# Moving V inside one core: a queue change, a transpose on TensorE, and a new placement of steps in a fused window-attention and MLP kernel

## The chip, the cores and the metric

The kernel runs on one core of a Trainium2 chip. The metric is the device time of one execution in microseconds (us); lower is better. Three executions of the kernel before took 382.96, 375.05 and 378.85 us, median 378.85 us. The profile shown below is of a separate, profiled execution with a span of 377.6 us.

## The reference

Eight batches of attention (8 heads, 576 positions, head dimension 64) in which each position sees itself and the 63 positions before it; the result goes through two matrix products with `h - tanh(h)` between them.

```python
scores = scale * np.matmul(q, k.transpose(0, 1, 3, 2))
mask = (rel >= 0) & (rel < window)            # rel = i - j, window = 64
scores = np.where(mask, scores, -1000000000.0)
attn = softmax(scores)                        # written out in the original
x = np.matmul(attn, v).transpose(0, 2, 1, 3).reshape(B * S, H * D)   # 4608 x 512
h = x @ w_in                                  # 512 x 2048
g = h - np.tanh(h)
out = (g @ w_out).astype(np.float32)          # 2048 x 512
```

Inputs and output are float32; the kernel works in bf16 with float32 accumulation.

## The kernel before

The 4608 tokens are cut into nine chunks of 512. For each chunk c there are 16 "h" operations (`hp_mm`: four 128x512 matmuls into one PSUM bank, then a tanh on ScalarE, then a subtraction on VectorE) and 16 "y" operations (`yp_mm`: four matmuls of the second product; after each fourth one the result is stored). They are laid out by number in a table of **steps**; everything of the attention is hung into these steps by hand with `at(step, function, arguments)`. Each engine executes its own instructions in exactly the order in which the loop emits them.

```python
OPS = {}
for m in range(M):                                   # M = 16
    OPS[2 * m] = "h", 0, m
    OPS[32 + m] = "y", 0, m
    OPS[48 + m] = "h", 1, m
    OPS[66 + 2 * m if m < 15 else 95] = "h", 2, m
    OPS[63 + 2 * m if m > 1 else 64 + m] = "y", 1, m
    for c in range(3, NC):
        OPS[32 * c + 2 * m] = "h", c, m
        OPS[32 * c + 2 * m + 1] = "y", c - 1, m
# ... (cut)
for h in range(32 * NC + 32):
    op = OPS.get(h)
    # ... (cut: emit the matmuls of op, then:)
    for fn, args in items.pop(h, []):
        fn(*args)
    if op and op[0] == "h":
        g_sub(*op[1:])
```

A batch b (counted from 0, so the third to sixth batches are b = 2 to 5) has four pairs of heads; pair g = 4 b + pr. The parts for one pair are: load q, k and v from HBM (GpSimd's queue, which also converts to bf16), `cast` (a re-ordering copy), `tr` (TensorE transposes of q or k, six of 96x96, then copied out of PSUM by ScalarE and VectorE), `scores` or `hidden_scores` (with the exponential on ScalarE), masking, `pv` or `tile_pv` (the product with V), the normalisation into `xs`, and last the transpose of `xs` into `xT`, which the first product reads.

V needs two copies of each key block: the product for a window of 64 queries reads 128 keys, 64 old and 64 new, over 128 partitions. V is loaded to `vall`, copied to `vb` (`cast_v`), and then moved between partitions by DMA into `vw`, of which there are two, used by even and odd batches:

```python
def windows_v(b, j, eng):                 # both halves: 128 rows of 1040 bytes
    if j == 0:
        keys_v(b, 0, eng)
    else:
        eng.dma_start(out=vw[b % 2][:, j]..., in_=vb[8 * j - 8:8 * j + 8]...)

def keys_v(b, j, eng=nc.sync):            # the new half alone: 64 rows
    eng.dma_start(out=vw[b % 2][64:128, j]..., in_=vb[8 * j:8 * j + 8]...)

def shift_v(b, j0, j1, eng=nc.sync):      # the old half is the new half of the block before
    lo, hi = vw[b % 2][0:64, j0 + 1:j1 + 1], vw[b % 2][64:128, j0:j1]
    if eng is nc.vector:
        eng.tensor_copy(lo, hi)
    # ... (cut)
```

`xs` becomes `xT` in one of two ways:

```python
def x_tr(b, half, w0, w1, bank, eng=nc.vector):   # TensorE transposes, copied out by eng
    tp = ps[:, bank, :]...
    for w in range(w0, w1):
        nc.tensor.transpose(tp[:, w - w0, :], xs[b % 2][:, w, 2 * half:2 * half + 2, :]..., ident)
    # ... (cut: move(eng, chunk_tile(c)..., tp...), one copy for each chunk touched)

def x_dma(b):                                     # DMA transposes on SyncE's queue
    # ... (cut: one DMA for each chunk touched, transpose=True)
```

SyncE's queue carries the stores of the result, the moves of V from batch 2 on and the DMA transposes. GpSimd's queue carries the loads, most `cast`s and `cast_v` from batch 3 on. To hold loads back, GpSimd copies one element of `gT` (`pace(step)`), which waits for the subtraction of the last h operation before that step; everything later on GpSimd waits behind it.

The placement of batch 2 and of later batches before the change:

```python
at(47, cast_pair, 8, V)
at(48, cast_pair, 9, G)
at(49, lambda: [cast_v(2, pr, V) for pr in range(NP)])
at(50, lambda: [windows_v(2, j, Y) for j in range(NJ)])        # Y: SyncE's queue
# ... (cut)
for i, (g, p) in enumerate(((8, 58), (9, 59), (10, 61), (11, 63))):
    at(48 + 3 * i, tr, g, "q", 3, A, V)
    at(49 + 3 * i, tr, g, "k", 3, A)
    for j in range(3):
        at(50 + 3 * i + j, hidden_scores, g, j, 4 + (3 * i + j) % 2)
    at(p, tile_pv, g, (6, 7))
# ... (cut)
LOADS = {4: (63, 64, 72), 5: (96, 99, 102), 6: (124, 128, 114)}   # k, q, v
for g in range(3 * NP, B * NP):
    b, pr = divmod(g, NP)
    a = 8 * g - 52
    s = 32 * b - 4
    cv, ky = s - 72 + 5 * pr, s - 54
    if b == 3:
        a = (62, 67, 72, 76)[pr]
        cv, ky = 63 + pr, 67
    elif b == 4:
        a = (80, 87, 95, 102)[pr]
        cv, ky = 77 + 3 * pr, 88
    elif b == 5:
        cv, ky = 107 + 2 * pr, 114
    # ... (cut)
    at(cv, cast_v, b, pr)
    # ... (cut: casts before a, tr at a and a + 2, scores at a + 5, 7, 9, masking at a + 11)
    for i in range(3):
        at(a + 13 + i, pv, g, i)
    at(a + 15, norm, g)
    if pr == NP - 1:
        at(a + 16, x_dma, b)
    for j in range(NJ):
        if pr == 0:
            at(ky + j // 2, windows_v, b, j, Y)
```

Of the kernel before, what the change touches and what calls it, by code (L numbers as in the profile page):

```python
# [15 lines left out]
def kernel(  # L16
# [11 lines left out]
    NP = H // 2  # L28
    NJ = S // 64
# [26 lines left out]
    ps = psum.tile([128, 8, 512], F32, name="ps")  # L56
# [329 lines left out]

    def hp_mm(c, ms, split):

        outs = [ps[:, m % 3 if c < 2 else m % 2, :] for m in ms]
        for kis in ((0, 2), (1, 3)) if split else ((0, 1, 2, 3),):  # L390
            for m, hp in zip(ms, outs):
                for ki in kis:
                    nc.tensor.matmul(hp, w_in_tile(ki, m),  # L393
                                     chunk_tile(c)[:, :, ki % 2, 64 * (ki // 2):64 * (ki // 2) + 64],
                                     start=(ki == 0), stop=(ki == 3))
        for m, hp in zip(ms, outs):
            th = sm_pool.tile([128, TOK], F32, tag="th", name="th")
            nc.scalar.activation(th, hp, ACT.Tanh)  # L398
            HID[c, m] = hp, th
# [27 lines left out]
    for m in range(M):  # L427
        OPS[2 * m] = "h", 0, m
        OPS[32 + m] = "y", 0, m
        OPS[48 + m] = "h", 1, m  # L430
        OPS[66 + 2 * m if m < 15 else 95] = "h", 2, m
        OPS[63 + 2 * m if m > 1 else 64 + m] = "y", 1, m
        for c in range(3, NC):
            OPS[32 * c + 2 * m] = "h", c, m
            OPS[32 * c + 2 * m + 1] = "y", c - 1, m
        OPS[32 * NC + 2 * m + 1] = "y", NC - 1, m
# [3 lines left out]
    def at(h, fn, *args):  # L440
        items.setdefault(h, []).append((fn, args))
# [84 lines left out]
    at(34, more_constants)  # L526
    at(35, lambda: [keys_v(1, j, (G, Y)[j % 2]) for j in range(NJ)])
    at(35, load, 7, "q", G)
    for g in 8, 9, 10, 11:
        at(35, load, g, "k", G)  # L530
        at(35, load, g, "q", G)
        if g == 8:
            at(35, load_v_all, 2)
    at(36, cast_pair, 4, V)
    at(37, tr_rows, 4, "k", 3, V)
    at(38, tr_rows, 4, "q", 0, A)
# [36 lines left out]
        nc.scalar.activation(PT[g % NPT][:, 3 * grp:3 * grp + 3, :], sp, ACT.Exp, scale=scale)  # L573

    at(47, cast_pair, 8, V)
    at(48, cast_pair, 9, G)
    at(49, lambda: [cast_v(2, pr, V) for pr in range(NP)])
    at(50, lambda: [windows_v(2, j, Y) for j in range(NJ)])
    at(50, cast_pair, 10, G)
    at(52, cast_pair, 11, G)  # L580
    at(52, load_all, 3, "k")
    at(52, load_all, 3, "q")
    at(53, load_v_all, 3)
    for i, (g, p) in enumerate(((8, 58), (9, 59), (10, 61), (11, 63))):
        at(48 + 3 * i, tr, g, "q", 3, A, V)
        at(49 + 3 * i, tr, g, "k", 3, A)
        for j in range(3):
            at(50 + 3 * i + j, hidden_scores, g, j, 4 + (3 * i + j) % 2)
        at(p, tile_pv, g, (6, 7))
    at(62, x_tr, 2, 0, 0, 4, 4, V)  # L590
    at(62, x_tr, 2, 0, 4, 9, 5, A)
    at(65, x_tr, 2, 1, 0, 4, 3, V)
    at(65, x_tr, 2, 1, 4, 9, 4, A)
    for i in range(2):
        at(140 + 4 * i, more_zeros, i)

# [2 lines left out]
        last = ((b + 1) * NJ - 1)  # L599
        nc.gpsimd.tensor_copy(tick, chunk_tile(last // WPC)[0:1, last % WPC, 0, 0:1])  # L600

    LOADS = {4: (63, 64, 72), 5: (96, 99, 102), 6: (124, 128, 114)}
    for g in range(3 * NP, B * NP):
        b, pr = divmod(g, NP)
        a = 8 * g - 52
        s = 32 * b - 4
        cv, ky = s - 72 + 5 * pr, s - 54
        if b == 3:
            a = (62, 67, 72, 76)[pr]
            cv, ky = 63 + pr, 67  # L610
        elif b == 4:
            a = (80, 87, 95, 102)[pr]
            cv, ky = 77 + 3 * pr, 88
        elif b == 5:
            cv, ky = 107 + 2 * pr, 114
        elif b == 6:
            cv = 120 + 4 * pr
        at(cv, cast_v, b, pr)
        if b < 7:
            at(a - {3: 4, 5: 4}.get(b, 7), cast, g, "q")  # L620
            at(a, tr, g, "q", 3, A, V)
        else:
            at(a - 14, cast_q, g)
            at(a - 12, bounce, g, "q")
            at(a - 6, tr_dma, g, "q")
        if b < 7:
            at(a - {3: 3, 5: 6}.get(b, 5), cast, g, "k")
            at(a + 2, tr, g, "k", 3, A)
        else:
            at(a - 13, cast, g, "k")  # L630
            at(a - 11, bounce, g, "k")
            at(a - 5, tr_dma, g, "k")
        for i in range(3):
            at(a + 5 + 2 * i, scores, g, i, 4)
        at(a + 11, masking, g)
        for i in range(3):
            at(a + 13 + i, pv, g, i)
        at(a + 15, norm, g)
        if pr == NP - 1:
            at(a + 16, x_dma, b)  # L640
        for j in range(NJ):
            if pr == 0:
                at(ky + j // 2, windows_v, b, j, Y)
        if pr == 0:
            hk, hq, hv = LOADS.get(b, (s - 72, s - 68, s - 78))
            if b == 3:
                continue
            for h, f in (hv, (load_v_all, b)), (hq, (load_all, b, "q")), (hk, (load_all, b, "k")):
                at(h, pace, h)
                if b == 5:  # L650
                    at(h, behind_x, 3)
                at(h, *f)
# [50 lines left out]
```

The softmax here doesn't subtract the row's maximum and nothing guards it: scores larger than these inputs give would overflow.

## Time and profile before

| what | value |
|---|---|
| device time, median of three | 378.85 us |
| span of the profiled execution | 377.6 us |
| TensorE (PE) busy | 330.6 us, 88% |
| VectorE (DVE), ScalarE (ACT), GpSimd (POOL) busy | 199.5, 183.9, 103.5 us |
| mean TensorE clock granted in the span | 0.964 |
| PE busy from 65 to 103 us (38 us) | 29.60 us |
| PE busy from 103 to 157 us (54 us) | 41.28 us |
| PE busy from 157 to 199 us (42 us) | 34.76 us |
| PE busy from 199 to 282 us (83 us) | 79.34 us |

The three stretches up to 199 us are where batches 2 to 5 pass through the attention. The profile names an instruction by engine, line of the kernel and tiles: `PE L322` is the product with V of batches 0 to 2 (`tile_pv`), `PE L346` that of later batches (`pv`), `L393` is the first product, `L417` the second, `L267` the transposes of q and k, `vw<-vb` the moves of V. An arrow such as `<-DMA vw<-vb` behind an instruction says what ended the idle time before it. The clock is a share of full speed; at 0.5 every matmul takes twice as long.

The steps can be found in the timeline by counting the groups of four matmuls of L393 and L417: step 48 begins at 65.35 us, step 64 at 102.41, step 73 at 113.48, step 79 at 127.10, step 96 at 157.12, step 121 at 186.15.

### The profile page before, as it was taken

What the parts mean: (1) busy time and instruction counts of PE and PEld (TensorE: products, weight loads), DVE (VectorE), ACT (ScalarE), POOL (GpSimd) and SP (SyncE); (2) the same over time, 40 slices, a digit from 0 to 9 for tenths busy, and PEclk for the clock granted to TensorE, in tenths of its full rate; (3) what the DMA queues carried; (4) which work ended last, traced back from release to release, by engine and by line L of the source; (5) the groups of instructions that cost most, each with busy time, mean ns of one, the idle gap of its engine ahead of it and who ended that gap; (6) DMA issues with size and microseconds to landing.
All of it is one profiled execution on the core that took longest, in us unless ns stands there. A gap on an engine that the chain in (4) does not pass through costs nothing.

```text
span 377.6 us, 6190 instructions
## 1 busy us (share of the span) xinstructions
PE 330.6 (88%) x2402; PEld 178.9 (47%) x2402; DVE 199.5 (53%) x330; ACT 183.9 (49%) x332; POOL 103.5 (27%) x153
## 2 busy tenths in 40 slices
PE   7879896796896878699849999999699999999996
PEld 3645444353453444355425555555345544444442
DVE  4557658653634358466605677666466534343400
ACT  3546264582564355366515666665355344444321
POOL 8811373402173800053507435351000000000000
PEclk9999999897999699899988999999999999999999
DMA  9999999193098107595496869768971401001012
GB/s 163 168 204 211 176 192 173 16 224 70 2 170 158 36 5 131 105 150 96 70 201 96 159 109 157 143 105 156 200 190 57 91 29 58 28 28 57 28 56 85
DMA packets 54654, 42.98 MB, mean 114 GB/s; under 512 B 23232, under 2 KB 48320, under 8 KB 54624
## 3 DMA queue, kind: packets, MB, share of 16 engines
q0 software_dynamic: 20816, 18.73, 32.6%
q1 hardware_dynamic: 33456, 23.42, 27.2%
q10 hardware_dynamic: 352, 0.43, 0.5%
q8 instruction: 19, 0.31, 0.3%
q14 instruction: 11, 0.09, 0.1%
HBM read 36.70 MB, written 11.21 MB: 127 GB/s over the span
## 4 chain that ended last, share of the span: by engine, by line
PE 61%; DMA 20%; DVE 7%; POOL 4%; ACT 4%; issue 2%; SPq 1%; POOLq 0%; ACTq 0%; DVEq 0%
PE ps L417 26%; PE ps L393 26%; DMA vw<-vb 9%; DMA vall<-in_v_dram 7%; PE ps L334 3%; PE ps L346 2%; PE ps L267 2%; DVE gT L405 2%; DMA qall<-in_q_dram 2%; DMA kt<-kd 1%; DMA kall<-in_k_dram 1%; DVE qt L86 1%; DVE xs L357 1%; DVE vb L86 1%; ACT th L398 1%
## 5 line engine op out<-in xcount | busy, mean ns | idle before, releaser
L393 PE MATMUL ps<-xT,wi 128*128 128x512 bf16 x576 | 151.8, 392 | 1.1 <-DVE gT L405 0.8
L405 DVE TENSOR_TENSOR gT<-ps,th 128x512 bf16<-128x512 f32 x144 | 99.0, 691 | 97.9 <-ACT th L398 96.2
L417 PE MATMUL ps<-w_out_sb,gT 128*128 128x512 bf16 x576 | 147.0, 384 | 2.0 <-DVE gT L405 1.3
L398 ACT ACTIVATE th<-ps 128x512 f32<-128x512 f32 x144 | 85.6, 597 | 82.5 <-PE ps L393 79.8
L393 PEld LDWEIGHTS <-wi 128*128 128x128 bf16 x576 | 62.2, 115 | 48.8 <-issue 5.4
L417 PEld LDWEIGHTS <-gT 128*128 128x128 bf16 x576 | 54.2, 99 | 58.4 <-issue 4.8
L336 ACT ACTIVATE pt<-ps 128x384 bf16<-128x384 f32 x60 | 29.4, 490 | 47.0 <-PE ps L334 47.0
L346 PE MATMUL ps<-vw,pt 128*128 128x130 bf16 x180 | 21.4, 223 | 16.6 <-DMA vw<-vb 14.4
L86 POOL COPY vb<-vall 72x1024 bf16<-72x1024 bf16 x20 | 20.8, 1057 | 37.9 <-DMA out_dram<-ysb 13.8
L357 DVE TENSOR_TENSOR xs<-ps,rc 64x576 bf16<-64x576 f32 x40 | 30.2, 755 | 1.0
L422 ACT ACTIVATE ysb<-ps 128x512 f32<-128x512 f32 x36 | 21.5, 597 | 18.6 <-PE ps L417 18.5
L86 DVE COPY qt<-ps 64x576 bf16<-64x576 bf16 x20 | 15.2, 760 | 23.2 <-ACT qt L84 23.1
L346 PEld LDWEIGHTS <-pt 128*128 128x128 bf16 x180 | 15.0, 99 | 23.5 <-issue 6.6
L334 PE MATMUL ps<-qt,kt 128*128 128x128 bf16 x180 | 20.8, 227 | 5.4 <-DMA kt<-kd 3.7
L86 POOL COPY kb<-kall 96x768 bf16<-96x768 bf16 x23 | 19.2, 837 | 13.3 <-ACT pt L309 6.0
L334 PEld LDWEIGHTS <-kt 128*128 128x128 bf16 x180 | 14.2, 101 | 18.0 <-issue 8.8
L86 POOL COPY qb<-qall 96x768 bf16<-96x768 bf16 x19 | 15.9, 839 | 14.8 <-PE ps L267 9.4
L84 ACT ACTIVATE kt<-ps 128x576 bf16<-128x576 bf16 x20 | 13.0, 649 | 5.6 <-PE ps L267 5.6
L452 POOL COPY tick<-gT 1x1 bf16<-1x1 bf16 x12 | 2.2, 180 | 47.7 <-DVE gT L405 47.7
L340 DVE TENSOR_TENSOR pt<-pt,ps 128x1152 bf16<-128x1152 bf16 x20 | 14.9, 746 | 0.1
L84 ACT ACTIVATE qt<-ps 64x576 bf16<-64x576 bf16 x20 | 12.7, 636 | 3.8 <-PE ps L267 3.8
L309 ACT ACTIVATE pt<-ps 128x640 bf16<-128x640 f32 (+1 forms) x16 | 10.0, 649 | 5.4 <-PE ps L306 5.3
(79 smaller groups left out, 215.7 us busy)
## 6 DMA issues: line engine op xcount, KB each, us to landing
out_dram<-ysb SPq DMA_DIRECT2D x36, 256.0 KB
vw<-vb SPq DMA_DIRECT2D x48, 130.0 KB
vall<-in_v_dram POOLq DMA_DIRECT2D x7, 576.0 KB, 11.3
kall<-in_k_dram POOLq DMA_DIRECT2D x5, 576.0 KB, 6.0
qall<-in_q_dram POOLq DMA_DIRECT2D x5, 576.0 KB, 7.8
wi<-in_moe_w_in_dram POOLq DMA_DIRECT2D x2, 1024.0 KB, 12.8
w_out_sb<-in_moe_w_out_dram POOLq DMA_DIRECT2D x2, 1024.0 KB, 20.4
kall<-in_k_dram POOLq DMA_DIRECT2D x11, 144.0 KB, 11.0
```

Of the source, the lines that this page charges most:

```text
L84: nc.scalar.activation(o, i, ACT.Copy)
L86: eng.tensor_copy(o, i)
L334: nc.tensor.matmul(sp[:, i, :], kT[g % NR][:, 64 * j:64 * j + 128], qT[g % NR][:, :, 64 * j:64 * j + 64], start=True, stop=True)
L336: nc.scalar.activation(PT[g % NPT][:, 3 * grp:3 * grp + 3, :], sp, ACT.Exp, scale=scale)
L340: nc.vector.tensor_tensor(p, p, mask.unsqueeze(1).to_broadcast([128, 2 * NJ, 64]), ALU.mult)
L346: nc.tensor.matmul(ps[:, 5 + grp, 130 * i:130 * i + 130], PT[g % NPT][:, j, :], vw[b % 2][:, j, 2 * pr:2 * pr + 2, :], start=True, stop=True)
L357: nc.vector.tensor_tensor(xo[r, :, :, pr, :], ov[r, :, :, h, 0:D], rc[r].to_broadcast([64, 3, 3, 64]), ALU.mult)
L393: nc.tensor.matmul(hp, w_in_tile(ki, m), chunk_tile(c)[:, :, ki % 2, 64 * (ki // 2):64 * (ki // 2) + 64], start=(ki == 0), stop=(ki == 3))
L398: nc.scalar.activation(th, hp, ACT.Tanh)
L405: nc.vector.tensor_tensor(gT[c][:, m, :], hp, th, ALU.subtract)
L417: nc.tensor.matmul(yp, gT[c][:, m, s * 128:(s + 1) * 128], w_out_sb[:, m, :], start=(m == 0), stop=(m == M - 1))
L422: nc.scalar.activation(ysb, ps[:, yp_bank(c, s), :], ACT.Copy)
```

## The change

Batch 2: `cast_v` goes to step 48, directly followed by nine moves of the new half alone, in order on GpSimd's queue (G); the old half is made by two VectorE copies at steps 54 and 55. The casts of pair 9 go from GpSimd to VectorE. The transposes, scores and products of pairs 8 to 11 are spread differently, and the scores of every pair use banks 4, 5, 4. The load of V for batch 2 is put ahead of eight other loads. Batch 3: `cast_v` one step later, all nine moves of V at step 68 on GpSimd's queue; its `xs` is transposed by TensorE (`x_tr` at steps 85 and 86 for the first two pairs, 92 and 93 for the other two) in place of `x_dma` at step 92. Batch 4: its steps, its `cast_v`, its moves and its loads (steps 71 to 73 in place of 63, 64, 72) go later. Batch 5 keeps its steps. Batch 6: loads, `cast_v` and moves go later. To fit, chunk 1's y operations end two steps earlier and chunk 2's h operations start two steps later, with three h operations in a row at 93 to 95. The aim is that the moves of V have landed when the products with V come to read them.

```diff
-        outs = [ps[:, m % 3 if c < 2 else m % 2, :] for m in ms]
+        outs = [ps[:, m % 3 if c < 2 or (c, m) == (2, 14) else m % 2, :] for m in ms]
 ...
-        OPS[66 + 2 * m if m < 15 else 95] = "h", 2, m
-        OPS[63 + 2 * m if m > 1 else 64 + m] = "y", 1, m
+        OPS[68 + 2 * m if m < 13 else 80 + m] = "h", 2, m
+        OPS[61 + 2 * m if m > 3 else 64 + m] = "y", 1, m
 ...
+    at(35, load_v_all, 2)
     for g in 8, 9, 10, 11:
         at(35, load, g, "k", G)
         at(35, load, g, "q", G)
-        if g == 8:
-            at(35, load_v_all, 2)
 ...
-    at(48, cast_pair, 9, G)
-    at(49, lambda: [cast_v(2, pr, V) for pr in range(NP)])
-    at(50, lambda: [windows_v(2, j, Y) for j in range(NJ)])
-    at(50, cast_pair, 10, G)
+    at(48, lambda: [cast_v(2, pr, V) for pr in range(NP)])
+    at(48, lambda: [keys_v(2, j, G) for j in range(NJ)])
+    at(49, cast_pair, 9, V)
+    at(51, cast_pair, 10, G)
     at(52, cast_pair, 11, G)
-    at(52, load_all, 3, "k")
-    at(52, load_all, 3, "q")
+    at(53, load_all, 3, "k")
+    at(53, load_all, 3, "q")
     at(53, load_v_all, 3)
-    for i, (g, p) in enumerate(((8, 58), (9, 59), (10, 61), (11, 63))):
-        at(48 + 3 * i, tr, g, "q", 3, A, V)
-        at(49 + 3 * i, tr, g, "k", 3, A)
+    at(54, shift_dve, 2, 0)
+    at(55, shift_dve, 2, 4)
+    for g, tq, s0, p in (8, 48, 50, 57), (9, 51, 53, 59), (10, 56, 58, 62), (11, 59, 61, 65):
+        at(tq, tr, g, "q", 3, A, V)
+        at(tq + 1, tr, g, "k", 3, A)
         for j in range(3):
-            at(50 + 3 * i + j, hidden_scores, g, j, 4 + (3 * i + j) % 2)
+            at(s0 + j, hidden_scores, g, j, 4 + j % 2)
         at(p, tile_pv, g, (6, 7))
-    at(62, x_tr, 2, 0, 0, 4, 4, V)
-    at(62, x_tr, 2, 0, 4, 9, 5, A)
-    at(65, x_tr, 2, 1, 0, 4, 3, V)
-    at(65, x_tr, 2, 1, 4, 9, 4, A)
+    at(63, x_tr, 2, 0, 0, 4, 3, V)
+    at(64, x_tr, 2, 0, 4, 9, 3, A)
+    at(67, x_tr, 2, 1, 0, 4, 3, V)
+    at(67, x_tr, 2, 1, 4, 9, 4, A)
 ...
-    LOADS = {4: (63, 64, 72), 5: (96, 99, 102), 6: (124, 128, 114)}
+    LOADS = {4: (71, 72, 73), 5: (96, 99, 102), 6: (126, 130, 122)}
 ...
-            a = (62, 67, 72, 76)[pr]
-            cv, ky = 63 + pr, 67
+            a = (64, 69, 73, 76)[pr]
+            cv, ky = 64 + pr, 68
         elif b == 4:
-            a = (80, 87, 95, 102)[pr]
-            cv, ky = 77 + 3 * pr, 88
+            a = (86, 95, 100, 105)[pr]
+            cv, ky = 88 + pr, 93
         elif b == 5:
             cv, ky = 107 + 2 * pr, 114
         elif b == 6:
-            cv = 120 + 4 * pr
+            cv, ky = 126 + 3 * pr, 138
         at(cv, cast_v, b, pr)
         if b < 7:
-            at(a - {3: 4, 5: 4}.get(b, 7), cast, g, "q")
+            at(a - {3: 4, 4: 4, 5: 4}.get(b, 7), cast, g, "q")
 ...
-            at(a - {3: 3, 5: 6}.get(b, 5), cast, g, "k")
+            at(a - {3: 3, 4: 5, 5: 6}.get(b, 5), cast, g, "k")
 ...
-        if pr == NP - 1:
+        if b == 3:
+            if pr % 2:
+                at(a + 16, x_tr, b, pr // 2, 0, 4, 3, V)
+                at(a + 17, x_tr, b, pr // 2, 4, 9, 3, A)
+        elif pr == NP - 1:
             at(a + 16, x_dma, b)
         for j in range(NJ):
             if pr == 0:
-                at(ky + j // 2, windows_v, b, j, Y)
+                at(ky + (0 if b == 3 else j // 2), windows_v, b, j, G if b == 3 else Y)
```

## The prediction

> **What bounds the kernel now.** I read the page's slices first: TensorE (PE) is busy 88% of the span, and its idle slices all lie in the first part and just after the middle; the last quarter is full.
>
> ```profile
> PE   7879896796896878699849999999699999999996
> PEclk9999999897999699899988999999999999999999
> ```
>
> A slice is 9.44 us. Digits of 6 to 8 between slice 6 and slice 21 are 57 to 200 us; the granted clock drops in the same places. Then the waits of PE say for whom:
>
> ```profile
> engine line waited for: us in total, times, longest us
> PE ps L346 <- DMA vw<-vb: 14.4, 7, 3.8
> PE ps L322 <- DMA vw<-vb: 3.7, 4, 1.8
> PE ps L334 <- DMA kt<-kd: 3.7, 2, 2.9
> PE ps L267 <- DVE qt L86: 3.0, 4, 1.9
> ```
>
> 18.1 us of PE's idle time waits for moves of V. Nothing else comes near. PE's timeline puts them in four places: 85.7 to 89.8 us (batch 2, 3.7 us), 119.7 to 124.5 (batch 3, 4.3 us), 153.0 to 156.8 (batch 4, 3.8 us) and 187.9 to 198.4 (batch 5, 1.69 + 1.94 + 2.73 = 6.4 us). Two of them:
>
> ```profile
> 87.74 0.22 PE L322 MATMUL ps<-vw,pt 128*64 128x65 bf16 x2 [1.83 <-DMA vw<-vb]
> ...
> 156.81 0.22 PE L346 MATMUL ps<-vw,pt 128*128 128x130 bf16 x1 [3.77 <-DMA vw<-vb]
> ```
>
> The busy time in windows set just behind these waits shows a second cost. Columns: window, length, busy time of PE, weight loads, DVE, ACT and GpSimd with counts, clock, DMA share, GB/s.
>
> ```profile
> 90.00:96.00 6.00, 6.00 (x46) 3.14 (x44) 3.29 (x6) 2.22 (x4) 1.81 (x2) 0.51 0.00 0
> ...
> 125.00:130.00 5.00, 5.00 (x22) 2.25 (x20) 3.01 (x5) 2.61 (x5) 5.00 (x6) 0.50 0.14 52
> ...
> 157.00:161.00 4.00, 4.00 (x25) 1.93 (x23) 3.85 (x7) 1.62 (x3) 0.49 (x3) 0.57 0.01 2
> ...
> 198.40:202.00 3.60, 3.60 (x18) 1.87 (x18) 1.88 (x4) 1.62 (x3) 3.31 (x5) 0.54 0.21 15
> ```
>
> PE is busy throughout, at half speed: lost work is length x (1 - clock), 6.0 x 0.49 = 2.9, 5.0 x 0.50 = 2.5, 4.0 x 0.43 = 1.7 and 3.6 x 0.46 = 1.7 us. In batch 5 a few more groups between the waits are slow (1.91, 0.53 and 1.40 us for what takes 1.03, 0.33 and 1.03 elsewhere), some 1.5 us.
>
> Last, why the moves are late, from the queues' timelines:
>
> ```profile
> 74.56 6.34 SPq L161 DMA_DIRECT2D vw<-vb  x8
> ...
> 149.70 2.93 SPq L378 DMA_TRANSPOSE xT<-xs  x2
> 153.16 0.60 SPq L161 DMA_DIRECT2D vw<-vb  x1
> ```
>
> ```profile
> 102.42 0.18 POOL L452 COPY tick<-gT 1x1 bf16<-1x1 bf16 x1 [10.49 <-DVE gT L405]
> ```
>
> Batch 2: moves issued to 80.9 us share the 16 engines with the loads of batch 3, issued from 72.43; the last is awaited until 89.75. Batch 3: GpSimd stands 10.49 us at a `pace` for batch 4's loads, with three of four `cast_v` behind it, so the moves begin at 108.17. Batch 4: the ninth move waits behind the DMA transposes of batch 3. Batch 5: the same, and V itself was late (its load was issued at 168.61, its first copy began at 176.56, the moves at 182.15).
>
> **What the Trainium skill says.** "TensorE: Matmul & The Clock Gate", section "HAM oscillation — how this bites in real kernels": pauses of PE over about 3.4 us bring the half-speed clock back. The trace agrees in the main: 3.77 us idle and then 0.57; it also shows 0.51 after four shorter waits of 3.7 us together. "DMA: Bandwidth & Descriptors", section "Anatomy of one DMA — SWDGE (gpsimd) path": a wait for a semaphore is done by the issuing sequencer, before the DMA is given out; so everything behind it in that queue waits too. The trace agrees (the ninth move at 153.16). The same page, section "Issuing engines are not separate DMA queues": another queue brings no bandwidth. So batch 2 gains by moving earlier and by half the bytes (65 KB in place of 130), not by GpSimd's queue as such. "SBUF — State Buffer", section "Who interferes with whom": a fast VectorE copy and GpSimd shut each other out. The trace agrees: `cast_v` on DVE has a median of 0.425 us, but the four beside GpSimd's copies at 70.8 us took 2.97 together.
>
> **The change part by part.**
>
> Batch 2. DVE idles 3.17 us ahead of its first `qt` copy at 69.40, from 66.2. The four `cast_v` fit there: 4 x 0.425 = 1.7 to 2.97 us, done at 68 to 69.2. GpSimd then issues nine moves at 0.59 each, to about 74.5; moves of this kind landed 3.7 to 5.2 us after issue, so all have landed by 79.5. The two VectorE copies (0.70 each) come at steps 54 and 55 (77.8 and 79.2 us now), and `tile_pv` at step 57. No wait is left: gained 3.7 + 2.9 = 6.6 us. The 1.4 us of copies lie in DVE's slack.
>
> Batch 3. GpSimd reaches its loads some 5 us later (nine issues in front), about 77.8; with no moves beside them they take about 14 us (8 us for a single V load, 6 each for k and q, overlapping), so V is there at about 92. Four `cast_v` at 1.05 plus four casts at 0.83 come to 7.5, less two casts done while V is awaited: moves from about 98, nine at 0.6 to 0.8, to 105, landed by 110. `pv` of pair 12 is now at steps 77 to 79. If step 64 comes at 94 and the 13 steps take 14.6 us as now (102.41 to 117.06), that is 108.6 to 111. Just enough. Gained 4.3 + 2.5 = 6.8, less about 1 for a wait of the transposes of pair 14, whose casts stand behind the moves on GpSimd.
>
> Batch 4. No transposes in SyncE's way. Moves are free to go after the last store of chunk 1 (step 92), nine at 0.75 = 6.8 us plus about 4.5 to land; `pv` at steps 99 to 101, some 9 to 11.5 us after step 92. Gained 3.8 + 1.7 = 5.5, less about 1.5 us as the last three may be late.
>
> Batch 5. It keeps its steps, but the transposes of batch 4 are now at step 121, behind all nine moves, the V load for batch 6 (issued at 182.43, in the middle of the moves) goes to step 122, and the pace at step 96 ends sooner: today it waits until 160.30, 3.2 us after step 96, since DVE stood behind batch 4's late `pv`. The moves then start some 22 us after step 96 in place of 25, and end at 28.5, landed at 33; `pv` 121 to 123 come 29 to 31 after. About 2 us of wait are left and 0.8 of slow clock. Gained 6.4 + 1.5 + 1.7 - 2.8 = 6.8 us.
>
> Added work: 18 transposes of 128x128; nine take 0.67 us in the trace, 0.51 from start to start with the next: 1.1 us on PE. Their copies are on DVE and ACT, which have slack. Bank 3 serves two halves of `x_tr` and the transposes of pair 12 at steps 63 and 64, one copy (0.4 to 0.7 us) after another: about 1.3 us. Pairs 12 to 15 are now 5, 4 and 3 steps apart in place of 5, 5 and 4, so `pv` meets the normalisation before it (0.22 + 2 x 0.755 us), and `x_tr` at 92 waits for the last one: about 1.5 us.
>
> Sum: 6.6 + 5.8 + 4.0 + 6.8 = 23.2, less 1.1 + 1.3 + 1.5 = 3.9, is 19.3. 378.85 - 19.3 = 359.6; I say 360. From step 121 on I expect no difference in what each step takes: the waits for `kt<-kd` (3.7 us) stay.
>
> **The rivals.** First, another engine takes over. From step 48 to 64 ACT has 16 tanh at 0.597, 12 exponentials at 0.49, 8 copies at 0.64: 20.6 us, and PE's work there is about 22 us at full clock, in 37.06 us. So ACT would bound only after 14 us were gained; but at a given step it can come last (banks 4, 5, 4 make the next pair's first scores wait for an exponential). That would take 2 to 4 us and give 363. Second, the wait moves from V to GpSimd: it now has 18 moves to issue in front of casts and loads, 5 us more before batch 3's loads. If V lands at 96, `pv` of batch 3 waits as before: 367. In favour: GpSimd already starved PE once by its order; against: it stood idle 9.38 us before 84.34 and 10.49 before 102.42. Third, the DMA engines: loads of batch 5 at step 96 meet batch 4's moves, and batch 4's wait stays: 365. Fourth, the clock drop after 125 or 198 goes away entirely and the residual waits vanish too: 352. That the wait is hidden anyway I exclude: PE is the chain behind 202 us, so each step that comes sooner ends sooner.
>
> **Range and chances.** 28.4 us (18.1 + 8.8 + 1.5) is all that the four waits cost; with nothing given back but the 1.1 us of transposes the time is 351.5. With the second and third rivals together it is about 371. Range 351 to 370. The executions of before spread by 1% to each side, which blurs the 2% line at 371.3. Faster by over 2%: 0.86; within 2%: 0.11; slower: 0.03.
>
> **What would show it.** PE waits for `vw<-vb` under 4 us in all (18.1 now), none in `tile_pv`; the first store or h group of chunk 3 at about 141 us (157.12 now); clock of 0.5 at no more than two places after 80 us. Wrong would be: a wait of more than 2 us of PE for a cast or a load (`kb`, `qb`), moves on GpSimd issued slower than 0.8 us each, or `pv` of batch 4 or 5 waiting as long as today.

## The result, and the profile after

The changed kernel takes 364.94 us (median of four executions, 363.63 to 365.60), the kernel before 380.35 (four, 375.05 to 382.96): ratio 0.968, 95% interval 0.958 to 0.977. In every comparison of this document executions that the chip disturbed as a whole are left out; the profiles of two experiments, e9 and e12, are of such executions, so only their times are used.

The slices of the page after (9.1 us each) answer to those of before:

```profile
PE   7679998699999779979689998897999999999995
PEclk9999999989999999989989999999999999999999
```

Of the dip from 57 to 103 us only the slices up to 73 us are left. Six slices had a low clock; now three have, at 73, 155 and 182 us. Digits of 6 and 7 stand at 118 to 136 us and at 155 to 182: batches 3 and 5 still leave marks. Who PE waits for, from the waits of the page after (in total, times, longest, in us):

```profile
PE ps L267 <- DVE qt L86: 3.3, 5, 1.9
PE ps L267 <- POOL qb L86: 3.2, 2, 2.2
PE ps L346 <- DMA vw<-vb: 2.5, 2, 1.9
PE ps L334 <- DMA kt<-kd: 2.4, 2, 2.2
...
PE ps L393 <- DMA xT<-xs: 1.8, 1, 1.8
```

The moves of V cost 2.5 us in place of 18.1, and `tile_pv` (L322) waits for none. Two entries are new: a cast of q on GpSimd (3.2) and the DMA transposes of x (1.8).

For a sum, cut both timelines at the same steps: 48, 64, 96, 124 and, as the last bound, 160. The windows of before, and then of after (columns as in the prediction; busy time and count of PE come first, the clock is the third figure from the right):

```profile
65.35:102.41 37.06, 28.66 (x258) 16.44 (x256) 20.89 (x35) 20.72 (x41) 7.75 (x10) 0.86 0.44 79
102.41:157.12 54.71, 41.99 (x305) 23.31 (x305) 26.30 (x42) 26.10 (x50) 19.18 (x25) 0.94 0.59 105
157.12:198.74 41.62, 34.38 (x230) 18.80 (x228) 22.43 (x36) 19.40 (x36) 14.04 (x23) 0.91 0.70 118
198.74:238.13 39.39, 39.39 (x282) 22.28 (x281) 26.72 (x42) 25.13 (x46) 20.38 (x27) 0.96 0.82 134
```

```profile
66.91:94.49 27.58, 23.89 (x227) 14.27 (x225) 20.09 (x36) 19.26 (x37) 14.77 (x21) 0.94 0.61 89
94.49:140.24 45.75, 39.54 (x329) 22.85 (x327) 26.55 (x43) 26.23 (x54) 22.45 (x33) 1.00 0.53 94
140.24:181.37 41.13, 34.61 (x257) 19.75 (x255) 24.32 (x38) 21.98 (x42) 15.51 (x24) 0.96 0.76 113
181.37:224.23 42.86, 39.96 (x283) 22.22 (x280) 26.77 (x42) 25.23 (x46) 19.50 (x26) 0.96 0.91 144
```

| steps | before, us | after, us | gain | PE idle before | PE idle after |
|---|---|---|---|---|---|
| 48 to 64 | 37.06 | 27.58 | 9.48 | 8.40 | 3.69 |
| 64 to 96 | 54.71 | 45.75 | 8.96 | 12.72 | 6.21 |
| 96 to 124 | 41.62 | 41.13 | 0.49 | 7.24 | 6.52 |
| 124 to 160 | 39.39 | 42.86 | -3.45 | 0 | 2.90 |

(What follows step 160 takes the same in both to 0.2 us.) Steps 48 to 96 bring 18.4 us; after that 3 us are lost again. Counted from step 48 the gain is 312.25 - 296.98 = 15.3 us, which is what the medians show (15.4). The spans differ by 13.7 only, as the profiled execution of before reached step 48 at 65.35 us and that of after at 66.91. Up to there the two programs differ only in the order of nine loads at step 35, and e8, which has the order of before, reached step 48 at 67.55, so this difference is not put down to the change.

The batch 5 stretch is the one to look at. PE's timeline of after, and GpSimd's:

```profile
157.86 0.66 PE L267 MATMUL ps<-ident,qb 96*128 96x96 bf16 x6 [2.17 <-POOL qb L86]
158.32 1.91 PE L417 MATMUL ps<-w_out_sb,gT 128*128 128x512 bf16 x4
...
181.15 0.22 PE L346 MATMUL ps<-vw,pt 128*128 128x130 bf16 x1 [1.93 <-DMA vw<-vb]
...
189.16 1.05 PE L393 MATMUL ps<-xT,wi 128*128 128x512 bf16 x4 [1.81 <-DMA xT<-xs]
```

```profile
143.17 0.18 POOL L452 COPY tick<-gT 1x1 bf16<-1x1 bf16 x1 [14.79 <-DVE gT L405]
...
143.75 0.78 POOL L103 DMA_DIRECT2D kall<-in_k_dram  x1 [0.17 <-issue]
...
146.18 0.77 POOL L103 DMA_DIRECT2D qall<-in_q_dram  x1
...
147.72 0.82 POOL L86 COPY qb<-qall 96x768 bf16<-96x768 bf16 x1
153.40 0.82 POOL L86 COPY kb<-kall 96x768 bf16<-96x768 bf16 x1 [4.86 <-PE ps L393]
...
154.53 0.84 POOL L146 DMA_DIRECT2D vall<-in_v_dram  x1
156.98 0.82 POOL L86 COPY qb<-qall 96x768 bf16<-96x768 bf16 x1 [1.62 <-DMA qall<-in_q_dram]
```

GpSimd was free from 148.54 on, but the first cast of batch 5's k starts at 153.40, 0.12 us after its load landed. (The releaser that the line names had long been done.) That load was issued at 143.75, landed at 153.28 and so took 9.5 us, that of q 10.7 (146.18 to 156.93). In the kernel before they took 5.8 and 6.3. The load of V stands behind the cast of k, so it went out at 154.53. What ran beside these loads is in SyncE's timeline of after:

```profile
136.05 0.63 SPq L176 DMA_DIRECT2D vw<-vb  x1
136.78 7.23 SPq L161 DMA_DIRECT2D vw<-vb  x8
...
168.58 0.64 SPq L176 DMA_DIRECT2D vw<-vb  x1
...
177.58 9.72 SPq L378 DMA_TRANSPOSE xT<-xs  x2
```

The first two lines are batch 4's nine moves, given out from 136.05 to 144.01 us behind the last store of chunk 1, though the last `cast_v` had ended at 126.8; the line at 168.58 is the first of batch 5's. And the two DMA transposes of batch 4's x take 9.7 us beside the load of V for batch 6 (issued 177.24, landed 188.65); step 128 waits for them. This gave the theory: the moves of batch 4 are 9 us later than they could be, and batch 5's loads pay. The rivals: the time is lost through GpSimd's or SyncE's order of issue as such, or through the new steps.

### The profile page after: what moved, and what is told of

Read it like the earlier page. It is cut to its first block, busy times and chain, and to the rows that moved or that the text cites. A ratio compares the mean times of both kernels' runs of the same rounds, so it can differ in the third digit from the quotient of the medians.

```text
span 363.9 us, 6219 instructions
## 1 busy us (share of the span) xinstructions
PE 326.4 (90%) x2420; PEld 178.1 (49%) x2420; DVE 200.7 (55%) x336; ACT 185.5 (51%) x336; POOL 111.2 (31%) x169
## 4 chain that ended last, share of the span: by engine, by line
PE 66%; DMA 10%; DVE 10%; ACT 5%; issue 4%; POOL 3%; SPq 0%; ACTq 0%; POOLq 0%; DVEq 0%
PE ps L393 29%; PE ps L417 27%; DMA xT<-xs 3%; DVE xs L357 2%; PE ps L267 2%; DMA vw<-vb 2%; PE ps L346 2%; PE ps L334 2%; ACT th L398 2%; DMA kall<-in_k_dram 2%; DVE qt L86 2%; DVE gT L405 2%; DMA kt<-kd 2%; DMA kf<-in_k_dram 1%; PE ps L363 1%
## 5 line engine op out<-in xcount | busy, mean ns | idle before, releaser
L393 PE MATMUL ps<-xT,wi 128*128 128x512 bf16 x576 | 147.6, 383 | 3.0 <-DMA xT<-xs 1.8
L393 PEld LDWEIGHTS <-wi 128*128 128x128 bf16 x576 | 61.2, 114 | 49.3 <-issue 3.2
L86 POOL COPY qb<-qall 96x768 bf16<-96x768 bf16 x18 | 15.1, 837 | 18.9 <-DMA qall<-in_q_dram 11.3
L86 POOL COPY kb<-kall 96x768 bf16<-96x768 bf16 x22 | 18.4, 839 | 7.4 <-PE ps L393 4.9
L334 PEld LDWEIGHTS <-kt 128*128 128x128 bf16 x180 | 13.9, 99 | 12.3 <-issue 4.2
L176 POOL DMA_DIRECT2D vw<-vb x20 | 11.6, 601 | 9.5 <-PE ps L393 6.7
L267 PE MATMUL ps<-ident,qb 96*128 96x96 bf16 x120 | 9.1, 215 | 4.8 <-POOL qb L86 3.2
## 6 DMA issues: line engine op xcount, KB each, us to landing
vall<-in_v_dram POOLq DMA_DIRECT2D x7, 576.0 KB, 11.4
```

The source lines that it names most:

```text
L86: eng.tensor_copy(o, i)
L267: nc.tensor.transpose(tp[:, e, :], src[:, e, :], ident[:P, :P])
L334: nc.tensor.matmul(sp[:, i, :], kT[g % NR][:, 64 * j:64 * j + 128], qT[g % NR][:, :, 64 * j:64 * j + 64], start=True, stop=True)
L393: nc.tensor.matmul(hp, w_in_tile(ki, m), chunk_tile(c)[:, :, ki % 2, 64 * (ki // 2):64 * (ki // 2) + 64], start=(ki == 0), stop=(ki == 3))
```

## The experiments

All are edits of the changed kernel, but e8, which is of the one before. Times of chosen steps, in us from step 48, counted in PE's timeline as the prediction's are:

| step | before | e8 | after | e1 | e2 | e3 | e4 | e5 | e7 | e10 | e11 |
|---|---|---|---|---|---|---|---|---|---|---|---|
| 64 | 37.06 | 36.44 | 27.58 | 27.38 | 27.67 | 30.94 | 27.48 | 26.47 | 26.47 | 27.74 | 27.57 |
| 80 | 63.77 | 57.42 | 49.20 | 49.00 | 51.50 | 52.56 | 49.11 | 48.09 | 48.09 | 49.36 | 49.19 |
| 96 | 91.77 | 89.03 | 73.33 | 73.11 | 76.51 | 76.67 | 70.87 | 73.76 | 72.21 | 73.48 | 73.31 |
| 104 | 101.89 | 99.54 | 82.85 | 82.49 | 85.89 | 86.06 | 91.14 | 85.15 | 81.59 | 82.86 | 83.41 |
| 109 | 107.61 | 105.26 | 91.41 | 88.51 | 95.07 | 94.84 | 97.17 | 91.17 | 87.83 | 92.07 | 89.43 |
| 124 | 133.39 | 131.36 | 114.46 | 108.84 | 118.20 | 115.81 | 116.70 | 112.93 | 107.87 | 113.87 | 109.83 |
| 128 | 138.98 | 136.91 | 122.25 | 115.09 | 125.42 | 121.30 | 120.85 | 120.08 | 112.02 | 121.45 | 113.98 |
| 160 | 172.78 | 170.71 | 157.32 | 153.30 | 160.59 | 157.90 | 158.45 | 155.69 | 156.93 | 158.63 | 148.40 |
| end | 312.25 | 309.40 | 296.98 | 293.17 | 301.14 | 298.79 | 298.84 | 296.71 | 296.58 | 298.15 | 287.99 |

### e1: the moves of batch 4 early

```diff
-            cv, ky = 88 + pr, 93
+            cv, ky = 84 + pr, 88
 ...
-                at(ky + (0 if b == 3 else j // 2), windows_v, b, j, G if b == 3 else Y)
+                at(ky + (0 if b in (3, 4) else j // 2), windows_v, b, j, G if b == 3 else Y)
```

> Batch 4's copies of V at steps 84 to 87 and all nine of its moves at step 88, ahead of the last store of chunk 1. Theory (the loads of k and q for batch 5, 143.75 and 146.18 to 153.28 and 156.93 us in the changed kernel, are slow because batch 4's moves of 136 to 144 us share the DMA engines with them): these loads land in 6 to 7 us as in the kernel before, the 2.17 us wait of TensorE for a cast of q at step 109 and the half clock behind it go, V of batch 5 is loaded about 4 us earlier and the 2.5 us of waits for its moves shrink below 1; gain 4 to 7 us on the changed kernel's 364.9, so 358 to 361. Rival A (GpSimd's own order or the paces hold these loads): the loads still take over 9 us, the wait stays, 364 to 366. Rival B (moves at 128 us meet the stores or come before the copies are done): batch 4's products wait, 366 or more.

Measured: 361.70 us, ratio 0.953 (0.947 to 0.959), just above the forecast. The moves went out from 125.27 to 133.30. GpSimd's timeline of e1 in the same place:

```profile
149.64 0.82 POOL L86 COPY kb<-kall 96x768 bf16<-96x768 bf16 x1 [1.17 <-DMA kall<-in_k_dram]
...
150.77 0.84 POOL L146 DMA_DIRECT2D vall<-in_v_dram  x1
152.47 0.82 POOL L86 COPY qb<-qall 96x768 bf16<-96x768 bf16 x1 [0.86 <-DMA qall<-in_q_dram]
```

The load of k, issued at 143.69 as before, took 5.8 us (landed 149.52), that of q 6.3, and V's went out 3.8 us sooner. PE's wait at 157.86 is gone, with the slow clock behind it, and `vw` costs 0.9 us in all. The stretch from step 96 to 124, columns as in the windows above:

```profile
140.18:175.91 35.73, 32.68 (x257) 18.92 (x255) 24.23 (x38) 21.85 (x42) 15.51 (x24) 1.00 0.64 106
```

It takes 35.73 us where after takes 41.13: 5.4 us from nothing but the place of nine moves and of the four copies ahead of them, with no byte less. The loads went out at the same times in both, so they were slow because of the moves. By step 128 e1 is 7.2 us ahead; at the end 3.8 are left, since between steps 128 and 160 it loses 3.1 (a wait of 1.85 us for a cast of q, again with the half clock behind it, where GpSimd stands 9.79 us at a `cast_v` of batch 7 for the moves of batch 6).

### e2 and e10: batch 3's moves on SyncE's queue

```diff
-                at(ky + (0 if b == 3 else j // 2), windows_v, b, j, G if b == 3 else Y)
+                at(ky + (0 if b == 3 else j // 2), windows_v, b, j, Y)
```

> Batch 3's nine moves at step 68 as in the changed kernel, but on SyncE's queue. Theory (the order counts, not the queue: SyncE is free at that step and the copies of V are no longer behind a pace): step 80 comes within 1 us of the changed kernel's and no wait for the moves of V appears in batch 3; 363 to 366. Rival (GpSimd's queue itself is quicker or in better order): moves land later, a wait of 2 us or more at steps 77 to 79, 367 to 370.

Measured: 369.37 us, ratio 0.972 (0.966 to 0.978). V was ready at 97.6 us. SyncE's timeline of e2:

```profile
102.57 0.33 SPq L424 DMA_DIRECT2D out_dram<-ysb  x1
103.09 0.63 SPq L176 DMA_DIRECT2D vw<-vb  x1
103.81 7.77 SPq L161 DMA_DIRECT2D vw<-vb  x8
```

The moves stood behind a store of chunk 1 that went out at 102.57; at step 77 PE waits 1.37 + 0.40 us for them, and step 80 comes 2.3 us later than in after. The theory (no wait for V, 363 to 366) failed, and the time is in the rival's range. Is it the queue or the store? e10 lets the moves go one step earlier (67), ahead of that store, with `cast_v` at 63 to 66:

```diff
-            cv, ky = 64 + pr, 68
+            cv, ky = 63 + pr, 68
 ...
-                at(ky + (0 if b == 3 else j // 2), windows_v, b, j, G if b == 3 else Y)
+                at(ky - 1 if b == 3 else ky + j // 2, windows_v, b, j, Y)
```

> Batch 3's moves on SyncE's queue at step 67 again, now with the copies of V at steps 63 to 66, so that all four stand ahead of the moves. (In the experiment before, the fourth copy stood behind the moves and had to wait for them.) Theory (order, not queue): moves start at 97 to 98 us, no wait at steps 72 to 80, step 80 at 49 to 49.7 us after step 48, batch 4 and 5 as in the changed kernel; 364 to 366. Rival (SyncE's slower giving out, 0.86 against 0.52 us a move): the last moves land at 110 us or later and TensorE waits 1 us or more at steps 77 to 79; 366 to 369.

Measured: 367.66 us, ratio 0.965 (0.958 to 0.972). SyncE's timeline of e10:

```profile
98.49 0.63 SPq L176 DMA_DIRECT2D vw<-vb  x1
99.21 7.21 SPq L161 DMA_DIRECT2D vw<-vb  x8
```

Step 80 comes at 49.36, in after at 49.20: no wait for V, as the theory had it, though the time as a whole lies in the rival's range. So for batch 3 it is the order in the queue that counts, not whose queue it is, although GpSimd gives out eight moves in 4.21 us and SyncE in 7.21. What e10 loses comes later (4.3 us of waits for casts of q and 3.3 for the transposes of x, in after 3.2 and 1.8) and is less than its interval settles. e6 had tried the same with `cast_v` left at 64 to 67: there the fourth pair's copy stands behind the moves in the program, so they do not wait for it and batch 3 computes with that pair's old V; and GpSimd's copy stands 11.97 us behind the moves.

> Batch 3's moves on SyncE's queue, one step earlier (67), so that they stand ahead of the first store of chunk 1 instead of behind it; all else as changed. Theory (the loss of the second experiment, 2.2 us at steps 77 to 80, came of the store that SyncE had to wait for until 102.6 us, while V had been ready at 97.6): moves start at 97 to 98 us, no wait at steps 77 to 80, step 80 at 49 to 49.5 us after step 48 as in the changed kernel; 364 to 366. Rival (SyncE gives out a move of 128 rows only every 0.86 us against 0.52 on GpSimd, so the last moves land late and meet batch 4's loads): a wait of 1 us or more remains at steps 77 to 80, and batch 5 suffers too, 366 to 369.

It took 370.08 us, ratio 0.975 (0.966 to 0.984), with no wait for V at steps 77 to 80, though step 80 came 1.7 us later than in after, mostly for a cast of q (1.38) behind that copy. As its dependences are others, it decides nothing; e10 does.

### e3: batch 2's moves as before, on SyncE and with both halves

```diff
-    at(48, lambda: [keys_v(2, j, G) for j in range(NJ)])
+    at(48, lambda: [windows_v(2, j, Y) for j in range(NJ)])
 ...
-    at(54, shift_dve, 2, 0)
-    at(55, shift_dve, 2, 4)
```

> Batch 2 moved by nine full moves (130 KB each after the first) on SyncE's queue at step 48, without the two VectorE copies; all else as changed. Theory (half the bytes and the place ahead of batch 3's loads make the gain of batch 2; GpSimd's loads now go out 5 us earlier and share the engines with twice the bytes): the last moves land at about 85 us, TensorE waits 1 to 3 us at the first product of batch 2 (step 57), step 64 comes 1 to 5 us later than in the changed kernel; 366 to 369. Rival (the earlier copy of V at step 48 alone makes the gain): no wait, step 64 within 0.5 us, 364 to 365.

Measured: 367.3 us (two executions, 367.01 and 367.57), ratio 0.968 (0.961 to 0.975); in the trace 1.8 us longer than after. SyncE needs from 69.69 to 78.60 us for the nine, and the loads of batch 3 start at 74.07. PE's timeline of e3:

```profile
85.08 0.22 PE L322 MATMUL ps<-vw,pt 128*64 128x65 bf16 x2 [0.77 <-DMA vw<-vb]
86.26 0.25 PE L322 MATMUL ps<-vw,pt 128*64 128x65 bf16 x4 [0.97 <-DMA vw<-vb]
```

Step 64 comes 3.4 us later. Of batch 2's 9.5 us, 6.1 come therefore from the rest of the change (the earlier `cast_v` and load of V, the new steps), and 3.4 from the half moves and GpSimd's queue together. Their shares were not tried apart.

### e4 and e5: batch 3's x by DMA transposes again

```diff
-        if b == 3:
-            if pr % 2:
-                at(a + 16, x_tr, b, pr // 2, 0, 4, 3, V)
-                at(a + 17, x_tr, b, pr // 2, 4, 9, 3, A)
-        elif pr == NP - 1:
+        if pr == NP - 1:
             at(a + 16, x_dma, b)
```

> Batch 3's x by DMA transposes at step 92 as in the kernel before; all else as changed. Theory (the TensorE transposes cost 1.1 us of work and 2.7 us of waits for the normalisation and bank 3, but they keep batch 4's moves from standing behind transposes on SyncE): TensorE gains about 3 us before step 96 and loses 3 to 6 us in waits for batch 4's moves behind it, with batch 5's loads held longer; 365 to 369. Rival (batch 4's products at steps 99 to 101 have room enough): no wait for the moves, the cost of the transposes is saved, 361 to 363.

Measured: 367.99 us, ratio 0.972 (0.966 to 0.978). Step 96 comes 2.5 us sooner, so the 18 transposes and the waits around them cost that much. But SyncE's timeline and PE's of e4 show what they buy:

```profile
134.77 2.95 SPq L378 DMA_TRANSPOSE xT<-xs  x2
137.90 0.64 SPq L176 DMA_DIRECT2D vw<-vb  x1
138.65 9.30 SPq L161 DMA_DIRECT2D vw<-vb  x8
```

```profile
149.66 0.27 PE L346 MATMUL ps<-vw,pt 128*128 128x130 bf16 x1 [5.09 <-DMA vw<-vb]
```

The moves stand behind the transposes, and steps 99 to 104 take 17.4 us where after takes 5.8. With e1's early moves that order is turned round; e5 asks whether the TensorE transposes are needed then.

> Batch 4's copies and moves early (as in the first experiment) and batch 3's x by DMA transposes again, now behind the moves on SyncE's queue. Theory (with the moves ahead of them the DMA transposes no longer cost anything; they save 1.1 us of TensorE work and the waits of TensorE for the normalisation and for bank 3): step 96 comes 2 to 2.5 us earlier than in the first experiment, no wait for the moves of batch 4, against it a wait of up to 1 us for xT at the start of chunk 3; 359.5 to 361. Rival (TensorE transposes are needed, as the change has it: the transposes hold the loads of batch 5 longer and these come late): a wait of 2 us or more for a cast near step 109, 362 to 365.

Measured: 364.21 us, ratio 0.960 (0.951 to 0.969). My theory said that they were not, and it fell: the transposes now come last (136.16 to 140.3 us) and step 96 waits for them. PE's timeline of e5:

```profile
141.49 1.86 PE L393 MATMUL ps<-xT,wi 128*128 128x512 bf16 x4 [4.75 <-DMA xT<-xs]
```

Counted from step 48 it ends 3.5 us after e1 in the trace; the medians differ by 2.5 us, with intervals that overlap. So x by TensorE is worth its 2.5 us in either order, by the traces.

### e7: later pieces behind batch 4's x

e1, with the load of V for batch 6 made to wait until batch 4's x is transposed, and `cast_v` of batch 7 at steps 152 to 164:

```diff
+        elif b == 7:
+            cv = 152 + 4 * pr
 ...
+                if b == 6 and h == hv:
+                    at(h, behind_x, 4)
```

> The first experiment's kernel, with batch 6's load of V held behind the DMA transposes of batch 4's x, and batch 7's copies of V moved later (steps 152 to 164 in place of 148 to 163). Theory (the transposes take 9 us to land since that load shares the engines with them, so TensorE waits 1.9 us at step 128; and the first copy of V of batch 7 holds the later casts of batch 6 on GpSimd until the moves of batch 6 have landed, so TensorE waits 1.85 us for a cast of q): both waits go with the half clock behind the second, 3 to 5 us less than the first experiment's 361.7: 357 to 359. Rival (V of batch 6 now comes too late, or another cast takes its place): a new wait of batch 6 or 7, 360 to 362.

Measured: 366.10 us, ratio 0.966 (0.958 to 0.974). The wait for x at step 128 did go (steps 124 to 128 take 4.15 us, in e1 6.25), but V for batch 6 then landed at 187.45, and its `cast_v` held the casts behind it on GpSimd. PE's timeline of e7:

```profile
190.29 0.66 PE L267 MATMUL ps<-ident,qb 96*128 96x96 bf16 x6 [6.12 <-POOL qb L86]
```

The rival won, and by more than its 360 to 362: a wait moved from SyncE's queue to GpSimd's.

### e8: the later loads alone, in the kernel before

```diff
-    LOADS = {4: (63, 64, 72), 5: (96, 99, 102), 6: (124, 128, 114)}
+    LOADS = {4: (71, 72, 73), 5: (96, 99, 102), 6: (124, 128, 114)}
```

> The kernel before with one number group of the change: batch 4's loads at steps 71 to 73 in place of 63, 64, 72, so that no pace stands ahead of the copies of V of batch 3 on GpSimd. Theory (the pace alone made batch 3's moves late): the copies of V are done at about 97 us, the moves on SyncE are out by 106, TensorE's wait of 4.3 us and the 2.5 us of half clock at steps 77 to 79 go; batch 2, 4 and 5 keep their waits; 372 to 375, less what batch 4's later loads cost. Rival (the bound of batch 3 is SyncE or the DMA engines): the wait stays over 2 us, 377 to 381.

Measured: 378.61 us, ratio 0.998 (0.995 to 1.002): no difference, and not the 372 to 375 of the theory. Yet the `pace` that held batch 3's `cast_v` is out of the way; the moves go at 98.79 us in place of 108.17, and steps 77 to 80 take 4.49 us in place of 10.43. Between steps 80 and 96 3.6 of these 5.9 us are given back: the loads of batch 4 are later (a wait of 1.88 us for its q) and its own moves still late; the waits for `vw<-vb` add up to 16.8 us. From step 48 to the end 2.85 us are left in this trace, which the medians do not show: the interval allows for 2 us at most. So removing one wait alone was worth little or nothing here.

### e9, e12 and e11: batch 6 later too, and half moves for batches 4 to 6

All three are e1 with batch 6's `cast_v` at 129 to 132 and its moves from 134. e9 has e7's edits besides; e12 has of them only `cast_v` of batch 7, and batch 6's moves all at one step. e11 is e12 with half moves for batches 4 to 6, still on SyncE's queue, and VectorE's copies for the other half:

```diff
+            at(ky + (0 if b in (3, 4, 6) else j // 2), keys_v if b in (4, 5, 6) else windows_v, b, j, G if b == 3 else Y)
 ...
+    for b, h in (4, 94), (5, 120), (6, 149):
+        at(h, shift_dve, b, 0)
+        at(h + 1, shift_dve, b, 4)
```

> The first experiment's kernel (batch 4's moves early), batch 6's load of V behind the DMA transposes of batch 4's x, its copies of V at steps 129 to 132, behind the cast of q of pair 23 and ahead of that of pair 24, its moves from step 134, and batch 7's copies of V at 152 to 164. Theory (in the third of the last set of experiments only the place of the first copy on GpSimd was wrong: it held a cast of q for 6.1 us): no wait for xT at step 128 and none over 1 us for a cast of q; step 136 at about 121 us after step 48 (123.6 in the first experiment), 356 to 359. Rival (V of batch 6 is now too late for its product at step 153): a wait of 2 us or more for moves of V near 207 us, 359 to 362.

> The same without the halved moves: the first experiment's kernel with batch 6's copies of V at steps 129 to 132 and moves at 134, batch 7's copies of V at 152 to 164. Theory (the place of the copies on GpSimd made the wait of 1.85 us for a cast of q near step 158, and the transposes of batch 4's x still share the engines with batch 6's load of V): the wait for xT at step 128 stays at 1.9 us, the wait for the cast goes with its half clock; 358 to 360. Rival (what waits is set by the DMA engines, not by the order on GpSimd): another wait of 2 us or more takes its place between steps 136 and 168, 361 to 363.

> The first experiment's kernel, with batches 4 to 6 moved as batch 2 is in the changed kernel (the new half by DMA on SyncE's queue, 65 KB a move, the old half by two VectorE copies at steps 94 and 95, 120 and 121, 149 and 150), batch 6's copies of V at steps 129 to 132 and moves at 134, batch 7's copies of V at 152 to 164. Theory (from 157 to 200 us the DMA engines are the scarce thing, and what waits behind them changes with each placement; half the bytes of the moves lets loads and transposes land sooner, while VectorE has room for 1.4 us a batch): V of batch 6 lands 1 to 2 us sooner, the waits for xT at step 128 and for casts of q or k of batch 6 stay below 1 us each; 3 to 6 us less than the first experiment's 361.7, 355.5 to 358.5, and at least 1.5 us below the other kernel of this set. Rival (VectorE now stands in its order at the copies of step 120 until the moves have landed, and holds subtractions and banks): new waits for VectorE of 2 us or more near step 121, 359 to 363.

Measured: e9 359.4 us, ratio 0.945 (0.941 to 0.950); e12 362.8, ratio 0.952 (0.944 to 0.961); e11 356.3, ratio 0.940 (0.933 to 0.947). e11 is the fastest version, some 2.8% below after. e9 and e12 lie above their forecasts (356 to 359, 358 to 360) and in their rivals' ranges, e9 by 0.4 us; e11 is in its own (355.5 to 358.5). The windows of 60 us in which batches 5 and 6 are loaded, of after, of e1 and of e11:

```profile
140.00:200.00 60.00, 51.66 (x371) 29.09 (x369) 35.53 (x55) 32.25 (x61) 21.13 (x32) 0.94 0.84 125
```

```profile
140.00:200.00 60.00, 54.99 (x420) 31.40 (x418) 40.25 (x63) 36.82 (x69) 26.01 (x39) 1.00 0.71 112
```

```profile
140.00:200.00 60.00, 56.33 (x427) 32.36 (x425) 43.15 (x67) 37.53 (x71) 28.85 (x41) 1.00 0.67 113
```

The DMA engines are busy 0.67 of the time in place of 0.84 and PE 56.33 us at full clock in place of 51.66 at 0.94; most of both is e1's already (0.71 and 54.99). SyncE's DMA transposes, 9.72 us in after and 6.52 in e1, take 2.84, and PE waits for none of them. How much of this last step is due to the half moves is not shown, as e12's trace is left out. The slices and the first waits of e11:

```profile
PEclk9999999989999999999999999999999999999999
```

```profile
PE ps L267 <- DVE qt L86: 3.3, 5, 1.9
PE ps L334 <- DMA kt<-kd: 2.5, 2, 2.2
PE ps L346 <- DVE xs L357: 2.4, 2, 1.4
```

No wait for V is among them. e11 against e12, which differ by the half moves (and their copies) alone, is 0.940 against 0.952: about 5 us, and the intervals overlap a little, so the size is uncertain. e9 and e11 can't be told apart by their intervals.

## Why the prediction was right, and where it was not

The time, 364.94, lies in the range and 5 us above the 360. By the parts, in its order:

- **The waits for V (right).** 2.5 us in all, none in `tile_pv`; batch 2's moves had landed by 77.9 us (predicted 79.5), batch 3's went out from 97.7 to 102.4 and had landed by 108.4 (98 to 105, and 110); step 64 came at 94.49 (94), step 96 at 140.24 (141). One reading was off, to no harm: 117.06 us is the first product of pair 12 at step 75 of the kernel before, not step 77. The 13 steps take 16.3 us there and 17.0 after, so that this product came at 112.3 and not at 108.6 to 111, which left the moves more room. GpSimd issued moves at 0.52 to 0.60 us.
- **Why they had been late (right, by e2, e3, e8 and e10).** A queue does its work in order: behind a `pace` (e8: moves at 98.79 without it, 108.17 with it), a store (e2: at 103.09, V ready at 97.6), a transpose (e4: at 137.90). e10 shows for batch 3 that GpSimd's queue is not what matters, as said; for batch 2 it was not tried apart from the half moves.
- **The added costs (right in kind, wrong as a subtraction).** I took off 3.9 us for transposes, bank 3 and waits for the normalisation. These waits are there: 0.82 + 0.29 + 0.68 + 0.93 + 1.41 = 4.1 us at the transposes and `pv` of batch 3, and 0.85 for bank 3. But PE's idle time for anything but V from step 48 to 96 was 21.1 - 11.8 = 9.3 us before and is 9.9 after. They took the place of others. Counted to step 96, the prediction's parts add up to 12.3 us (11.8 of waits for V and 5.4 of slow clock, less 1.0 and 3.9); the runs brought 18.4. By an estimate from PE's busy time inside the slow stretches of both traces, these are 11.8 of waits for V, 6.0 of slow clock (7.5 before, 1.5 after) and 1.2 less work, less 0.6 of other waits. The work is less, in spite of the transposes, as some 2 us of batch 4 now lie behind step 96 (PE's count there rose from 230 to 257). The prediction did not agree with itself here: steps 64 and 96 at 94 and 141 us mean 8.4 and 16.1 us gained, close to what came (7.9 and 16.9 by the same clock times), its parts 6.6 and 12.3.
- **The step that failed: "Batch 5 ... Gained 6.8 us".** Measured from step 96 to 124: 0.49. (By its parts 6.1 belong there: 0.9 of the 6.8 lie behind step 124, and 0.2 of batch 4's part ahead of it.) What I had not put in: 2.17 us of waiting for a cast of q, 1.0 for a normalisation, the clock at 0.60 from 157.86 to 162 us (1.7 us), and batch 4's moved work (about 2: PE is busy here for 32.68 us at full clock in e1, and was for 34.38 less 0.09 x 41.62, or about 30.6, before). The slow clock behind the last wait, 0.64 from 181 to 186 us, costs 1.7 us as before, where I allowed 0.8. The cause is the third rival the other way round: I asked what batch 5's loads would do to batch 4's moves, and not what the moves would do to the loads. Moving batch 4 later put nine 130 KB moves onto 576 KB loads. e1 undoes that alone and gets 5.4 us back. A sign that I had named for being wrong did come: a wait of more than 2 us for a cast.
- **The wait left for V in batch 5 (right in size, by luck).** It was 0.61 + 1.93 us, and "about 2" was foreseen. But the moves started 28.3 us after step 96 (168.58), not 22: the `pace` there, which I expected to end some 3 us sooner, still ended 2.9 us after the step (143.17; 3.2 before), and the loads were slow. The wait stayed small only because the products were late too: step 121 came 33.7 us after step 96 and not 29.
- **"From step 121 on I expect no difference" (wrong by 3.5 us).** Batch 4's DMA transposes now run beside the load of V for batch 6: 1.81 us at step 128; and PE waits 1.08 us for a cast of q at 220.95. These are the 2.90 us of idle time in the last window; of the other 0.55 some 0.2 are clock and the rest is PE's work. e7 shows that the first wait goes when the load waits, and in e11 neither is there.
- **The kept waits for `kt<-kd`.** 2.4 us against 3.7; that they stay is right, and e1, e2 and e4 show 2.4, 2.6 and 3.5.

The sum, by the same three stretches: 12.3 + 6.1 + 0.9 = 19.3 was predicted, and 18.4 + 0.5 - 3.5 = 15.4 measured. Two errors, of 6 and of 10 us, partly cancelled; that the total came within 5 us is in part luck. So is it that the third rival's number, 365, came true: its wait, of batch 4 for its moves, did not come.

## What to carry to other kernels

A wait that is removed early in a kernel brings its gain only if what stands behind it keeps its transfers apart: for every DMA that a change moves, look up which loads it will run beside, and count the delay on both sides. Ask also whose order in the queue holds a transfer: put the early, ready ones ahead of a store or a transpose that waits for its data. When transfers collide, sending half the bytes and letting an idle engine copy the rest is worth trying.

## What the runs showed of the hardware that was not expected

- One short pause can be enough for the slow clock, but need not be. After's windows ahead of and behind the 2.17 us wait for q, the slow stretch alone, and the time behind the 2.25 us wait for `kt<-kd` that ended at 254.10:

```profile
153.00:155.70 2.70, 2.69 (x22) 1.50 (x20) 2.12 (x3) 2.01 (x5) 1.91 (x4) 1.00 0.92 192
155.70:157.86 2.16, 0.00 (x0) 0.00 (x1) 0.00 (x0) 0.52 (x1) 0.82 (x1) 0.98 0.56 73
157.86:162.00 4.14, 4.14 (x24) 2.42 (x25) 1.45 (x2) 1.13 (x2) 0.00 (x0) 0.60 0.69 112
...
157.78:161.19 3.41, 3.33 (x18) 1.96 (x19) 1.45 (x2) 0.92 (x2) 0.02 (x1) 0.50 0.83 135
...
254.10:258.10 4.00, 4.00 (x28) 2.33 (x29) 2.08 (x4) 2.10 (x4) 0.00 (x0) 1.00 0.93 232
```

  PE was busy throughout before the wait for q, and yet the clock behind it is 0.60 for 4.1 us; behind the longer wait it is 1.00, as it is behind the 1.81 us at step 128. In the traces of before and after every slow stretch, but the one that the span cuts off at the end, lasts 3.41 us or twice that (157.78 to 161.19 above; 89.05 to 95.88 and 123.19 to 130.02 in before). Why one pause brings such a stretch and another does not is not shown. The section "HAM oscillation — how this bites in real kernels" of the Trainium skill's page "TensorE: Matmul & The Clock Gate" puts this at pauses over about 3.4 us; here the measurement decides: 2.17 us cost 1.7 more.
- The time to give out a move differs by queue: eight full moves take 4.21 us on GpSimd (batch 3 in after) and 6.34 to 9.30 on SyncE (batch 2 in before, batch 4 in e4); nine half moves take SyncE 6.49 (batch 4 in e11). The Trainium skill ("DMA: Bandwidth & Descriptors", section "Issuing engines are not separate DMA queues") calls the time saved by another issuing engine usually small beside the DMA itself. For batch 3 it is 3 us over eight moves (7.21 in e10 against 4.21), and it did not show in the steps: step 80 came 0.16 us later.
- Batch 5's loads of k and q (576 KB each) landed 5.8 and 6.3 us after issue in before and in e1, 9.5 and 10.7 in after, beside the moves of V. The load of V for batch 6 took 11.4 beside the DMA transposes in after, that for batch 5, without them, 8.4.
- Four `cast_v` on VectorE took 1.43 us in after, where GpSimd copied nothing at the time, and 2.97 in before, beside its copies.
